# Decode layers with cached attention: the 32-key blocks of K and V in another order over the partitions

## The chip, the core and the metric

The kernel runs on one core of one Trainium2 chip. The metric is the device time of one execution in microseconds (us); a kernel's time is the median of several executions. Durations of single instructions, waits and transfers come from one profiled execution, whose own time stands beside its span below.

## What is computed

Four tokens (B = 4, one new token for each of four sequences, D = 512) go through two identical pairs of layers. The first layer of a pair is attention over a cache: 32 query heads share 8 key/value heads (4 queries to one), each with Sk = 4096 cached keys and values of width Dh = 128. The second is a gated feed-forward layer of width 1792.

```python
def _A_ref(x, k_cache, v_cache, wq, wo):
    q = (x @ wq).reshape(B, Sq, Hq, Dh).transpose(0, 2, 1, 3)
    k = jnp.repeat(k_cache, rep, axis=1)
    v = jnp.repeat(v_cache, rep, axis=1)
    scores = jnp.einsum("bhqd,bhkd->bhqk", q, k) * (Dh ** -0.5)
    p = _softmax(scores, axis=-1)
    o = jnp.einsum("bhqk,bhkd->bhqd", p, v)
    return o.transpose(0, 2, 1, 3).reshape(B, Sq, Hq * Dh) @ wo

x = x + _A_ref(_layernorm(x), k_cache, v_cache, wq, wo)
x = x + _B_ref(_layernorm(x), w_gate, w_up, w_down)
# and the same two lines once more, with the same weights and caches
```

Everything is bf16 in DRAM. K and V of one sequence and one key/value head are 4096 x 128 numbers, 1 MB each. Over the four sequences and eight heads K is 32 MB and V is 32 MB.

The softmax and the sum over the values run over all 4096 keys, so the keys of one head may stand in any order, as long as K and V use the same one.

## The kernel before

K is read from DRAM once and used for both attention layers; V is read twice, once for each attention layer. The work on a head follows one pattern:

- One load brings the 1 MB of a head into one place of `KV`, a buffer of 11 places (`SLOTS`, line 22 and line 337). A place has 128 partitions of 4096 bf16 numbers, 8 KB each: partition p gets 32 consecutive keys, which is one run of 8 KB in DRAM. The keys 32p to 32p+31 are called block p here.
- VectorE transposes the K head in place, in 32 x 32 blocks (`turn`, line 393, its instruction on line 396).
- TensorE computes scores for four heads into one bank of PSUM (`scores`, line 411, its matmuls on line 418). VectorE and ScalarE make the softmax of them (lines 427 to 474), and the probabilities end in `PT` with the same assignment of keys to partitions as K and V have.
- TensorE sums the values (`values`, line 502, its matmuls on line 509), 32 matmuls for a head: each contracts over the 128 partitions, so over 128 blocks, with one key of each.

Heads come by one of two loaders, both of which issue on SyncE's queue. `ld_head` (line 376, the issue on line 379) loads a whole head: 128 partitions of 8 KB. `ld_half` (line 382, the issue on line 385) loads the first or the second 16 keys of each block: 128 partitions of 4 KB out of the 8 KB. All K heads and 16 of the V heads come whole, 48 loads of 1 MB; the other V heads come in halves, 96 loads of 512 KB. For both, the partition is the slowest dimension on both sides of the copy, with 128 entries.

The order of everything is worked out before the program is built. The class `Plan` holds each operation with an engine, a duration, what it needs and what it frees; `loads_k` (line 919) and `loads_v` (line 929) add the loads in a fixed order; `pl.run` (line 1200) chooses the order of issue and the place in `KV` for each load from constants (microseconds per KB and the like). A load is issued when the readers of what stood in its place are done. `spin` (line 1197) fills TensorE's planned gaps with matmuls whose results are not used. None of the plan's inputs says which key goes to which partition.

The last four V heads go to the space of `wq_sb`, which is no longer needed then. At the end come the last output projection, the last feed-forward layer and the stores, about 11 us after the last head has landed.

Of the kernel before, what the change touches and what calls it, by code (L numbers as in the profile page):

```python
# [14 lines left out]
P = 128  # L15
# [36 lines left out]
class Plan:  # L52
# [7 lines left out]
    def add(self, name, eng, dur, deps, emit, acq=(), rel=(), soft=()):  # L60
        assert name not in self.nodes, name
        self.nodes[name] = dict(eng=eng, dur=dur, deps=[d for d in deps if d is not None],
                                emit=emit, acq=acq, rel=rel, soft=list(soft))
        return name
# [191 lines left out]
def kernel(  # L256
# [13 lines left out]
    nc = tc.nc  # L270
# [78 lines left out]
    for z in range(2):  # L349
# [3 lines left out]
                          in_=fold[:].unsqueeze(1).broadcast_to([P, 4, 32]))  # L353
# [9 lines left out]
    def slot(pick):  # L363
        place, h = pick
        whole = wq_sb[:, place[1], :] if isinstance(place, tuple) else KV[:, place, :]
        return whole if h is None else whole[:, 2048 * h:2048 * h + 2048]
# [5 lines left out]
    where = {}  # L372

    def ld_head(name, src):
        def emit(pick):
            where[name] = slot(pick)
            nc.sync.dma_start(out=where[name], in_=src.rearrange("(p c) d -> p (c d)", p=P))
        return emit  # L380

    def ld_half(name, h, src):
        def emit(pick):
            where[name, h] = slot(pick)
            nc.sync.dma_start(out=where[name, h], in_=src.rearrange("(p c) d -> p (c d)", p=P)[:, 2048 * h:2048 * h + 2048])
        return emit

    def keys(name, h):
# [301 lines left out]
    def qtwo_split(z):  # L690
        def emit():
            t = big[:, 256 * z:256 * z + 256].rearrange("p (h x) -> p x h", x=32)
            q = qc[:, z].rearrange("p (f h) -> p f h", f=2)
            nc.vector.scalar_tensor_tensor(out=q, in0=t[:, 2:4], scalar=mneg, in1=t[:, 0:2],
                                           op0=ALU.mult, op1=ALU.add)
            nc.vector.tensor_tensor(out=qs[:, 64 * z:64 * z + 64].rearrange("p (j h) -> p j h", j=4),
                                    in0=qc[:, z:z + 1].broadcast_to([P, 4, 16]),
                                    in1=mask_i.unsqueeze(2).broadcast_to([P, 4, 16]), op=ALU.mult)
        return emit
# [20 lines left out]
    def qsplit(z, b):  # L720
        def emit():
            q = qr[:, z].rearrange("p (k x e) -> p x k e", x=32, e=2)[:, b:b + 1]
            nc.vector.tensor_tensor(out=qs[:, 64 * z:64 * z + 64].rearrange("p (j k e) -> p j k e", j=4, e=2),
                                    in0=q.broadcast_to([P, 4, 8, 2]),
                                    in1=mask_i.unsqueeze(2).unsqueeze(3).broadcast_to([P, 4, 8, 2]), op=ALU.mult)
        return emit
# [3 lines left out]
    def qrep(z):  # L730
        def emit():
            v = slice(64 * z, 64 * z + 64)
            nc.tensor.matmul(Qp[:, v], lhsT=rep[:], rhs=qs[:, v], start=True, stop=True)
        return emit
# [107 lines left out]
    def gelu_b(nb):  # L842
        def emit():
            u = ff(nb)[2]
            nc.scalar.activation(out=u, in_=u, func=ACT.Exp, scale=-2.0 * GELU_C * GELU_A)
            nc.scalar.activation(out=u, in_=u, func=ACT.Ln, bias=ones[:, 1:2])
            nc.scalar.activation(out=u, in_=u, func=ACT.Exp, scale=-1.0)
        return emit
# [25 lines left out]
    def gelu(nb):  # L874
        def emit():
            g = ff(nb)[1]
            nc.scalar.activation(out=g, in_=g, func=ACT.Gelu_apprx_tanh)
        return emit
# [40 lines left out]
    def loads_k(b):  # L919
        for j in range(8):  # L920
            soft = []
            if b and j >= 3:
                soft = [("sc", b - 1, 1, 0 if j < 7 else 1, 1)]
            elif b:
                soft = [("val", b - 2, 1, 5 + j) if b > 1 else ("val", 0, 0, 5 + j)]
            pl.load(("k", b, j), 8, ld_head(("k", b, j), A_k_cache[b, j]), [("sc", b, 1, j // 4, 1)],
                    soft=soft)

    def loads_v(b, L, j0=0, j1=8):
        n = AHEAD.get(b + 1, (0, 0))[1]  # L930
        for j in range(j0, j1):
            if L and j < n:
                soft = [("val", b + 1, 0, AHEAD[b + 1][0] - 3 + j)]
            elif L == 0:
                soft = [("val", b, 0, j - 3) if j >= 3 else (("sc", b - 1, 1, 1, 1) if b else None)]
            elif b == B - 1:
                soft = [("sc", b, 1, 0, 1)]
            else:
                soft = [("val", b + 1, 0, 5 + j - n) if j - n < 3 else ("val", b, 1, j - 3)]
            soft = [x for x in soft if x]  # L940
            name, src = ("v", b, L, j), A_v_cache[b, j]
            if halved(b, L, j):
                pl.load(("vh", b, L, j), 4, ld_half(name, 0, src), [("va", b, L, j)], soft=soft, half=0)
                pl.load(name, 4, ld_half(name, 1, src), [("val", b, L, j)], soft=soft, half=1)
            else:
                pl.load(name, 8, ld_head(name, src), [("val", b, L, j)], soft=soft)
# [97 lines left out]
    for b in range(B):  # L1044
        bs = slice(b, b + 1)
        for L in range(2):
            s = None
            for z in range(2):
                a = ("qx", b, L, z)
                if L:  # L1050
                    p = add(("qs", b, z), "DVE", 0.2 if b else 0.37, [("qt", b, z)], qsplit(z, 0) if b else qtwo_split(z),
                            rel=() if b else (f"big{z}",))
                    p = add(("qp", b, z), "PE", 0.2, [p], qrep(z), acq=("T1",) if z == 0 else ())
# [15 lines left out]
            for z in range(2):  # L1069
                e = (b, L, z)  # L1070
# [11 lines left out]
            if L == 0:  # L1082
# [14 lines left out]
                e = add(("gb", b), "ACT", 0.62, [a], gelu_b(1))  # L1097
# [13 lines left out]
    for b in range(B):  # L1111
        for L in range(2):
            for j in range(8):
# [8 lines left out]
                name, vals = ("v", b, L, j), values2 if pairs else values  # L1122
# [9 lines left out]
                for k, (t0, t1) in enumerate(cuts):  # L1132
                    if t != t1 - 1:
                        continue
                    e = (b, L, z, k)
# [21 lines left out]
    c = add("rowz", "DVE", 0.1, [("of", B - 1, 1, 1, 2)], rows_clear)  # L1157
# [13 lines left out]
    e = add("gset", "ACT", 1.3, [("lnr", "f2")], gelu_table)  # L1171
    e = add("gb2", "ACT", 0.25, [a, e], gelu(B))
    t1 = add("gy2", "DVE", 0.22, [t1], scaled(1, B, rs))
    a = add("gc2", "DVE", 0.22, [e, t1], gelu_c(B))
    c = add("rows", "DVE", 0.7, [end_x, c, a], rows)
# [42 lines left out]
    with tc.manual_schedule():  # L1218
        for name, pick in order:
            e = pl.nodes[name]["emit"]  # L1220
# [36 lines left out]
```

## Time and profile before

| what | value |
|---|---|
| median of 3 runs | 303.39 us (299.53 to 307.93) |
| profiled execution, its own time | 300.37 us |
| profiled execution, span from first to last instruction | 298.4 us |
| mean granted TensorE clock | 0.992 |
| TensorE matmul busy | 230.3 us, 77% (85.5 us of it the largest group of L1197, unused results) |
| VectorE busy | 167.6 us, 56% |
| ScalarE busy | 39.5 us, 13% |
| read from DRAM | 114.56 MB |

The span is the time between the first and the last instruction in the trace; 2.0 us of the execution's own time lie around it. In part 2 of the profile's page the span is cut into 40 equal slices, and each digit is the busy share of a slice in tenths. "SPq" is SyncE's queue, in which the loads are issued; "issue to landing" is the time from such an issue until all of the load's data are in place. "L379" is line 379.

### The profile page before, as it was taken

To read this page: it belongs to the slowest core of one execution; us is meant where nothing else is said; L and a number is where in the kernel's file an instruction comes from. 1 tells how busy PE (TensorE), PEld (TensorE's weight loads), DVE (VectorE), ACT (ScalarE), POOL (GpSimd) and SP (SyncE) were. 2 spreads that over 40 slices of the span, in tenths; PEclk is the share of its full clock that TensorE was granted. 3 is DMA by queue.
4 is the path that set the end of the run, shared out by engine and by line. 5 is a ranking of instruction groups with operands and counts; after the bars stand their busy time and mean duration, and the time that the engine had idled before them with its cause. 6 is when DMAs were issued, how large, how long until landed. Compare 5 with 4: busy or idle time off the path is not lost.

```text
span 298.4 us, 9206 instructions
## 1 busy us (share of the span) xinstructions
PE 230.3 (77%) x4164; PEld 106.4 (36%) x4164; DVE 167.6 (56%) x410; ACT 39.5 (13%) x94; POOL 0.7 (0%) x6
## 2 busy tenths in 40 slices
PE   0197668867896778899876788998777888997965
PEld 0122233322531334454322444454223444544433
DVE  4177963113479893164698941355989622555433
ACT  1020102001020301002203010012112010122102
POOL 0000000000000000000000000000000000000000
PEclk9997999999999999999999999999999999999999
DMA  7999999999989999999999999999999999999910
GB/s 303 404 423 422 421 406 422 399 430 418 419 323 426 376 412 406 405 406 408 380 421 405 406 404 402 406 408 412 408 408 401 412 407 409 404 389 424 419 79 3
DMA packets 23254, 115.15 MB, mean 386 GB/s; under 512 B 2992, under 2 KB 2992, under 8 KB 16560
## 3 DMA queue, kind: packets, MB, share of 16 engines
q1 hardware_dynamic: 23200, 114.57, 95.3%
q8 instruction: 32, 0.52, 0.7%
q14 instruction: 6, 0.05, 0.0%
q10 hardware_dynamic: 16, 0.00, 0.0%
HBM read 114.56 MB, written 0.00 MB: 384 GB/s over the span
## 4 chain that ended last, share of the span: by engine, by line
DMA 70%; PE 18%; DVE 7%; SPq 2%; issue 1%; ACT 0%; DVEq 0%; ACTq 0%
DMA KV<-in_A_v_cache_dram 54%; DMA KV<-in_A_k_cache_dram 8%; DMA wd_sb<-in_B_w_down_dram 7%; PE O_ps L509 5%; PE S_ps L418 4%; DVE KV L396 2%; PE S_ps L1197 2%; PE R_ps L654 2%; PE R_ps L771 1%; DVE big L554 1%; SPq L915 1%; DVE Qb L402 1%; PE S_ps L1190 1%; PE R_ps L809 1%; PE O_ps L563 1%
## 5 line engine op out<-in xcount | busy, mean ns | idle before, releaser
L1197 PE MATMUL S_ps<-iden_b 128*64 128x256 f32 (+5 forms) x238 | 85.5, 457 | 0.0
L396 DVE STREAM_TRANSPOSE KV<-KV 128x1024 int32<-128x1024 int32 x64 | 74.2, 1209 | 1.1 <-DMA KV<-in_A_k_cache_dram 1.0
L509 PE MATMUL O_ps<-KV,PT 128*4 128x128 bf16 x1856 | 43.9, 218 | 21.0 <-DMA KV<-in_A_v_cache_dram 19.6
L509 PEld LDWEIGHTS <-PT 128*4 128x4 bf16 x1920 | 31.9, 83 | 57.0 <-issue 47.0
L418 PE MATMUL S_ps<-KV,Qb 128*32 128x512 bf16 x512 | 38.3, 397 | 12.2 <-DVE KV L396 7.3
L554 DVE STREAM_TRANSPOSE big<-O_ps 128x128 f32<-128x128 f32 (+3 forms) x24 | 12.4, 516 | 45.2 <-PE O_ps L509 43.6
L1197 PEld LDWEIGHTS S_ps<-iden_b 128*64 128x64 f32 x238 | 24.9, 137 | 21.5 <-issue 12.0
L418 PEld LDWEIGHTS <-Qb 128*32 128x32 bf16 x512 | 14.0, 95 | 31.9 <-issue 12.0
L427 DVE TENSOR_REDUCE tiny<-S_ps 128x1 f32<-128x512 f32 x16 | 10.9, 682 | 13.2 <-PE S_ps L418 13.2
L449 ACT ACTIVATE big<-S_ps,bT 128x512 bf16<-128x512 f32 x8 | 5.5, 687 | 89.2 <-DVE bT L441 46.5
L645 ACT ACTIVATE lnt<-lnt 128x1 f32<-128x1 f32 (+1 forms) x10 | 2.0, 203 | 106.9 <-DVE lnt L638 93.2
L589 PE MATMUL R_ps<-XS,tiny 128*128 128x8 f32 (+1 forms) x16 | 3.3, 284 | 13.9 <-DVE XS L580 13.9
L1197 PE MATMUL T_ps<-iden_b 128*64 128x512 f32 (+2 forms) x30 | 13.4, 561 | 0.0
L771 PE MATMUL R_ps<-wo_sb,OT 128*1 128x512 bf16 (+1 forms) x152 | 10.4, 378 | 2.7 <-DMA wo_sb<-in_A_wo_dram 1.8
L466 PE MATMUL T_ps<-big,iden_b 128*32 128x128 bf16 x256 | 6.5, 220 | 7.8 <-DVE big L458 7.6
L474 ACT ACTIVATE PT<-T_ps 128x512 bf16<-128x512 f32 x16 | 9.6, 597 | 19.9 <-PE T_ps L466 15.7
L778 DVE STREAM_TRANSPOSE DA<-R_ps 128x512 f32<-128x512 f32 x8 | 5.7, 711 | 10.7 <-PE R_ps L771 10.7
L458 DVE STREAM_TRANSPOSE big<-big 128x256 int32<-128x256 int32 x16 | 7.0, 440 | 5.3 <-ACT big L449 5.1
L466 PEld LDWEIGHTS <-iden_b 128*32 128x32 bf16 x256 | 4.6, 96 | 14.8 <-issue 10.4
L654 PE MATMUL R_ps<-wq_sb,xz 128*1 128x512 bf16 (+1 forms) x128 | 9.7, 419 | 0.2 <-issue 0.2
L820 DVE STREAM_TRANSPOSE DA<-R_ps 128x448 f32<-128x448 f32 (+1 forms) x10 | 6.0, 601 | 5.2 <-PE R_ps L797 4.4
L449 ACT ACTIVATE big<-S_ps,bT,tiny 128x512 bf16<-128x512 f32 x8 | 6.2, 777 | 18.2 <-DVE bT L441 18.2
(124 smaller groups left out, 157.6 us busy)
## 6 DMA issues: line engine op xcount, KB each, us to landing
KV<-in_A_v_cache_dram SPq DMA_DIRECT2D x96, 512.0 KB, 7.2
KV<-in_A_k_cache_dram SPq DMA_DIRECT2D x32, 1024.0 KB, 12.3
KV<-in_A_v_cache_dram SPq DMA_DIRECT2D x12, 1024.0 KB, 13.4
wq_sb<-in_A_wq_dram SPq DMA_DIRECT2D x1, 4096.0 KB, 12.4
wo_sb<-in_A_wo_dram SPq DMA_DIRECT2D x2, 2048.0 KB, 24.0
wq_sb<-in_A_v_cache_dram SPq DMA_DIRECT2D x4, 1024.0 KB, 13.5
wg_sb<-in_B_w_gate_dram SPq DMA_DIRECT2D x1, 1792.0 KB
wu_sb<-in_B_w_up_dram SPq DMA_DIRECT2D x1, 1792.0 KB, 19.0
```

The costliest lines, as they stand in the source:

```text
L396: nc.vector.transpose(out=w, in_=w)
L418: nc.tensor.matmul(S_ps[z][32 * t:32 * t + 32], lhsT=Qb[:, z, at:at + 32], rhs=kw[t][:, 16 * m:16 * m + 16, je // 2, :, je % 2], start=(m ...
L427: nc.vector.tensor_reduce(out=cms[:, z:z + 1], in_=S_ps[z][:].rearrange("p c r -> p (c r)"), axis=AX.X, op=ALU.max)
L449: nc.scalar.activation(out=Pm[z].bitcast(BF16).rearrange("p (a r e) -> p a r e", a=8, e=2), in_=S_ps[z][:].rearrange("p (a e) r -> p a r e ...
L458: nc.vector.transpose(out=w, in_=w)
L466: nc.tensor.matmul(T_ps[z][32 * i:32 * i + 32, t].rearrange("p (a m x) -> p a m x", a=8, m=2), lhsT=iden_b[:, 32 * t:32 * t + 32], rhs=w[: ...
L474: nc.scalar.activation(out=PT[L][:, z].rearrange("p t a m h e -> p (t a m h e)"), in_=T_ps[z][:].rearrange("p t x -> p (t x)"), func=ACT.Copy)
L509: nc.tensor.matmul(o[32 * g:32 * g + 4, t, :], lhsT=PT[L][:, z, t, c // 2, h, :, c % 2], rhs=vw[:, c, :], start=(h == 0 and n == 0), stop= ...
L554: nc.vector.transpose(out=big[:, P * t0:P * t1].rearrange("p (t j m) -> p t j m", j=4, m=32), in_=o[:, t0:t1, :].rearrange("p t (m j) -> p ...
L654: nc.tensor.matmul(R_ps[z][32 * je:32 * je + nb, :], lhsT=xn[:, c, bs], rhs=w[:, 16 * z:16 * z + 16, je // 2, :, je % 2], start=(c == 0), ...
L771: nc.tensor.matmul(R_ps[0][t:t + nb, :], lhsT=src[:, k, :], rhs=w[:, k, :], start=(k < 4), stop=(k >= n - 4))
L1197: nc.tensor.matmul(sinks[place][0:64, 0:64 * n].rearrange("p (a n) -> p a n", a=n), lhsT=iden_w, rhs=iden_w.unsqueeze(1).broadcast_to([P, ...
```

## The change

Both loaders take the source through a new view, `blocks`. A head's 4096 keys are seen as 8 x 16 x 32 (i, e, c), and the partitions are counted with e outside and i inside: partition 8e + i gets block 16i + e. Partition 0 has block 0 as before, partition 1 has block 16, partition 7 has block 112, partition 8 has block 1, and so on. Each partition still gets one run of 8 KB, or the first or second 4 KB of it. K and V use the same view.

On the source's side the slowest dimension of the copy now has 16 entries (8 KB apart), the next has 8 (128 KB apart); on the side of `KV` there are 128 partitions as before. No instruction is added or taken away on any engine, and the plan is the same; the two issues move from lines 379 and 385 to lines 384 and 390.

```diff
+    def blocks(src):
+        return src.rearrange("(i e c) d -> e i (c d)", i=8, e=16)
+
     def ld_head(name, src):
         def emit(pick):
             where[name] = slot(pick)
-            nc.sync.dma_start(out=where[name], in_=src.rearrange("(p c) d -> p (c d)", p=P))
+            nc.sync.dma_start(out=where[name], in_=blocks(src))
         return emit
 
     def ld_half(name, h, src):
         def emit(pick):
             where[name, h] = slot(pick)
-            nc.sync.dma_start(out=where[name, h], in_=src.rearrange("(p c) d -> p (c d)", p=P)[:, 2048 * h:2048 * h + 2048])
+            nc.sync.dma_start(out=where[name, h], in_=blocks(src)[:, :, 2048 * h:2048 * h + 2048])
         return emit
```

## The prediction

> **What bounds the kernel now.** I read the page from its second part on: first the DMA rows of the 40 slices, then the queues of part 3.
>
> ```profile
> DMA  7999999999989999999999999999999999999910
> GB/s 303 404 423 422 421 406 422 399 430 418 419 323 426 376 412 406 405 406 408 380 421 405 406 404 402 406 408 412 408 408 401 412 407 409 404 389 424 419 79 3
> ...
> q1 hardware_dynamic: 23200, 114.57, 95.3%
> ```
>
> The reader is to see that the 16 DMA engines are busy from the second slice to the 38th, at 400 to 430 GB/s. Then the chain that ended last, part 4 of the page:
>
> ```profile
> DMA 70%; PE 18%; DVE 7%; SPq 2%; issue 1%; ACT 0%; DVEq 0%; ACTq 0%
> ```
>
> The chain is landing, matmuls, next issue, landing. Its PE pieces are the readers whose end frees a place, not a second bound: the engines go on with other queued loads under them. Part 6 gives the sizes.
>
> ```profile
> KV<-in_A_v_cache_dram SPq DMA_DIRECT2D x96, 512.0 KB, 7.2
> KV<-in_A_k_cache_dram SPq DMA_DIRECT2D x32, 1024.0 KB, 12.3
> KV<-in_A_v_cache_dram SPq DMA_DIRECT2D x12, 1024.0 KB, 13.4
> ...
> wq_sb<-in_A_v_cache_dram SPq DMA_DIRECT2D x4, 1024.0 KB, 13.5
> ```
>
> So 96 halves are 50.33 MB and 48 whole heads are 50.33 MB: 100.66 of 114.57 MB go through the two edited loaders. Now the busy time by stretches (the last three columns are granted clock, DMA share and GB/s): whole heads, a stretch where the queue runs thin, halves, the end.
>
> ```profile
> 15.00:35.00 20.00, 15.44 (x102) 4.88 (x102) 16.30 (x25) 3.48 (x7) 0.00 (x0) 0.91 1.01 422
> ...
> 83.00:105.00 22.00, 16.98 (x224) 6.42 (x215) 19.52 (x34) 4.35 (x10) 0.00 (x0) 1.00 0.95 374
> ...
> 165.00:195.00 30.00, 26.06 (x585) 13.40 (x570) 14.07 (x32) 2.38 (x6) 0.00 (x0) 1.00 1.02 405
> ...
> 280.00:298.40 18.40, 12.20 (x324) 6.55 (x323) 6.23 (x27) 1.94 (x4) 0.00 (x0) 0.97 0.28 113
> ```
>
> Whole heads run at 422 GB/s, halves at 405, both with no idle share: the engines are the bound there, about 26 GB/s for each of the 16. The last view is the DMA rows of a short early stretch, 3 to 13 us, with slices of 0.25 us, where `wq_sb` is loaded:
>
> ```profile
> DMA  0099900999039960399303993069900999002799
> GB/s 0 0 524 1180 393 0 0 655 1049 393 0 131 524 1180 262 0 131 655 1180 131 0 131 786 1049 131 0 262 1049 786 0 0 393 918 786 0 0 35 138 434 361
> ```
>
> A transfer is counted where it starts. The reader is to see pulses: the 16 engines begin their long rows nearly together, and for the rest of the period almost nothing begins. A load starts on all engines in step.
>
> **What the change does, part by part.**
>
> *Instructions.* None is added, removed or moved on any engine, and no wait changes. K and V are permuted alike, so scores, softmax and sums do the same work. Cost 0, with nothing needed to hide it.
>
> *Issue on SyncE's queue.* The source has three dimensions instead of two. The trace has these issues:
>
> ```profile
> L385 SPq DMA_DIRECT2D KV<-in_A_v_cache_dram x96: 327/328/791, 86.9 to 259.3; - x96
> ...
> 165.24 32.23 SPq L385 DMA_DIRECT2D KV<-in_A_v_cache_dram  x26
> ```
>
> (min, median and max in ns; then 26 issues in 32.23 us, one per 1.24 us.) The queue is occupied for 0.33 of 1.24 us and waits the rest. The nearest rows with three dimensions are the loads of `wo_sb` and `x_b`, 0.38 to 0.43 us an issue. Lower bound 0; upper, by the longest half's issue, 0.79 us, which still fits under 1.24 us, with seven loads more behind it. Not hidden are the issues in the chain itself (0.49, 0.33, 0.24, 0.60, 0.45 and 0.22 us, 2.3 in all): doubled, +2.3 us. I take 0, by the `wo_sb` rows.
>
> *The reading side.* [...] The gain is bounded by how far the loads are from the best rate in the page, the slice at 430 GB/s: all 100.66 MB at that rate take 234.1 us. Now they take 50.33 MB / 405 GB/s = 124.3 us and 50.33 / 422 = 119.3 us, 243.6 in all. So the gain is between 0 and 9.5 us. I take 0: K heads, with rows one behind the other, and the weights, with rows of up to 32 KB, move at much the same rate, so the order in DRAM does not look like what limits.
>
> *The writing side.* This is what I expect to decide. [...] Now the source counts 16 entries of 8 rows. If each engine takes one entry, as the change wants, engine e must write partitions 8e to 8e+7: the neighbours in DRAM are had by giving the engines other partitions. The trace of before shows only the old assignment, at a rate alike for 4 KB rows, 8 KB rows and weights, so a limit that is the same for all sources and may well lie on the writing side. A new assignment can then only keep that rate or lose it. Bounds from the rows: at best a row takes as long as now (+0). At worst two engines always write through one path and a row takes twice as long: +243.6 us.
>
> Between them: let two engines each write four rows over one path, then four over another. When both are on the same path each goes at half speed. If one leads by f rows, four rows take 8 - f row times: twice the time at f = 0, one and a half at f = 2, none lost at f = 4. Engines start a load in step (the pulses), which speaks for small f; over 150 loads the leads can drift, which speaks for more. I take the middle, f = 2: +0.5 x 243.6 = +121.8 us. Already idle DMA time pays a little back: in the stretch from 83 to 105 us the share is 0.95 where 1.02 is full, 0.07 x 22 = 1.5 us.
>
> [...]
>
> *The sum.* 300.37 + 0 + 0 + 121.8 - 1.5 = 420.7, so **421 us**, against the profiled execution's own 300.37 us (span 298.4, 2.0 around it). The median of the runs shown is 303.39, 1% above. The stretch after the last landing (280 to 298.4 us holds the last rows and some 11 us of compute) stays. When the loads take 1.5 times as long, TensorE, busy 77%, only waits more.
>
> **The rivals.**
>
> *No change.* The engines keep their partitions, or may write any partition at full rate, and the reading side is not the limit. For it: the flat rate over all kinds of source. Against it: to read neighbours together the engines must be given other partitions. Price 0 to +2.3 us (issues in the chain): 297 to 306 us with the scatter of the runs, 301 the likeliest. That the change does not do what it says (each engine keeps its old partitions and reads rows 128 KB apart) ends here too.
>
> *Faster.* DRAM order does cost today: halves, which leave out every other 4 KB, run at 405, whole heads at 422. If neighbours bring everything to 430 GB/s, 9.5 us go: 291 us, 3% less. It decides once all these loads run at 424 GB/s or more (100.66 MB in 237.6 us, 6.0 us or 2% less). Against it: the slices between 165 and 195 us, where halves alone are loaded, show 402 to 406, and whole heads no gain over the weights.
>
> *The issue becomes the bound.* If an issue with three dimensions takes more than a half's time on the engines (512 KB at 405 GB/s = 1.29 us), SyncE's queue sets the pace of 96 halves: at 1.5 us, 96 x 0.21 = 20 us, so 321 us. Against it: every three-dimensional issue in the trace takes under 0.45 us.
>
> *A write-side loss that is small.* Leads settle near f = 4: at f = 3.5 rows take 4.5/4, +30 us, 331 us. The two together are "slower, but little", 308 to 345 us.
>
> **How the numbers follow.** Large write-side loss: 0.62, its own range 349 us (f = 3.2, x1.2) to 543 us (x2). Slower by little: 0.12. No change: 0.18. Faster: 0.08. The prediction is the first's 421 us. The range goes from 298, which takes in nearly all of "no change", to 513 us (f = 0.5: 0.875 x 243.6 = +213 us); left out are "faster" and the top of the first case, under 0.2. Faster by over 2%: 0.08; within 2% (about what a measurement of this kernel, with 299.5 to 307.9 over three runs, can tell from none): 0.18; slower by over 2%: 0.74.
>
> **What would show it.** The DMA rows of the slices: still 9 everywhere, but 220 to 340 GB/s where K and V are loaded and still about 420 where `wo_sb`, `wg_sb` and `wu_sb` are (first 80 us). A share of 9 with fewer GB/s means rows that take longer; a share that falls means late issues, seen as longer issues on line 390. Issue to landing of halves would rise from 7.2 to 10 us and more. TensorE's granted clock may fall, as its waits lengthen. I am wrong if the rate of the halves stays at 405 GB/s or rises, and wrong in size if it leaves 220 to 340.

## The result and the profile after

| kernel | median | runs |
|---|---|---|
| before | 301.46 us | 299.53 to 307.93, 6 runs |
| changed | 450.6 us | 442.56 to 462.88, 6 runs |
| changed / before | 1.479 | 95% interval 1.471 to 1.488 |

The changed kernel takes half as long again. Its runs scatter by 4.6%; the ratio goes by those close to its fastest, and the profiled execution (462.88 us, span 461.0) is its slowest, so its stretches overstate the loss a little.

First the DMA rows of the 40 slices and the queue's row of the changed kernel's page, as they were shown of the kernel before. A slice is now 11.5 us.

```profile
DMA  9999999999999999999999999999999999999950
GB/s 364 220 227 228 227 293 229 232 406 334 240 233 231 257 256 260 269 272 260 248 242 248 261 252 250 247 248 249 242 252 264 267 280 275 266 248 235 233 144 2
...
q1 hardware_dynamic: 23200, 114.57, 97.4%
```

The engines are as busy as before (97.4% of 16 engines' span; 95.3% before), with the same 23200 packets and the same 114.57 MB, and move 220 to 280 GB/s where K and V alone are loaded. The peak of 406 in the ninth slice is the weights, which do not go through the new view. The engines do not run out of work: each transfer of K and V takes longer. By the single rows in the trace, a row of 8 KB takes 550 ns on average where it took 319, and one of 4 KB 251 where it took 164 (some rows of weights have these sizes and are counted in); the weights' rows of 32 KB take 1307 ns (1303 before). The chain and the loads:

```profile
DMA 89%; PE 9%; DVE 1%; SPq 1%; issue 0%
...
KV<-in_A_v_cache_dram SPq DMA_DIRECT2D x96, 512.0 KB, 11.7
KV<-in_A_k_cache_dram SPq DMA_DIRECT2D x32, 1024.0 KB, 24.3
KV<-in_A_v_cache_dram SPq DMA_DIRECT2D x12, 1024.0 KB, 18.9
```

The chain is now 89% DMA (70 before). Halves take 11.7 us from issue to landing (7.2 before), K heads 24.3 (12.3). The busy time by stretches (last three columns: granted TensorE clock, DMA share, GB/s), whole heads first, then a stretch with halves alone:

```profile
20.00:60.00 40.00, 15.50 (x105) 5.58 (x105) 19.41 (x25) 1.63 (x4) 0.00 (x0) 0.71 1.01 227
...
150.00:205.00 55.00, 36.27 (x666) 17.34 (x667) 15.01 (x38) 3.12 (x9) 0.00 (x0) 0.79 1.03 262
```

Whole heads run at 227 GB/s in the first stretch where they ran at 422, which makes a row take 1.86 times as long; halves at 262 in the second where they ran at 405, 1.55 times. TensorE's clock is 0.71 to 0.79 there. Last, the issues on SyncE's queue (duration in ns, min/median/max):

```profile
L390 SPq DMA_DIRECT2D KV<-in_A_v_cache_dram x96: 536/537/1523, 125.5 to 401.6; - x96
```

An issue takes 537 ns where it took 328.

### The profile page after: what moved, and what is told of

Same layout as the page of the kernel before. It is cut to its first block, busy times and chain, and to the rows that moved or that the text cites. A ratio compares the mean times of both kernels' runs of the same rounds, so it can differ in the third digit from the quotient of the medians.

```text
span 461.0 us, 9206 instructions
## 1 busy us (share of the span) xinstructions
PE 278.4 (60%) x4164; PEld 122.6 (27%) x4164; DVE 169.4 (37%) x410; ACT 39.4 (9%) x94; POOL 0.7 (0%) x6
## 3 DMA queue, kind: packets, MB, share of 16 engines
q1 hardware_dynamic: 23200, 114.57, 97.4%
## 4 chain that ended last, share of the span: by engine, by line
DMA 89%; PE 9%; DVE 1%; SPq 1%; issue 0%
DMA KV<-in_A_v_cache_dram 68%; DMA KV<-in_A_k_cache_dram 14%; DMA wd_sb<-in_B_w_down_dram 6%; PE O_ps L514 3%; PE S_ps L1202 1%; PE S_ps L423 1%; PE R_ps L673 1%; PE R_ps L814 1%; PE R_ps L659 1%; PE R_ps L776 0%; SPq L384 0%; PE R_ps L891 0%; DVE Qb L407 0%; DVE big L559 0%; PE R_ps L751 0%
## 5 line engine op out<-in xcount | busy, mean ns | idle before, releaser
L514 PE MATMUL O_ps<-KV,PT 128*4 128x128 bf16 x1856 | 52.3, 247 | 105.3 <-DMA KV<-in_A_v_cache_dram 104.2
L1202 PE MATMUL S_ps<-iden_b 128*64 128x256 f32 (+5 forms) x238 | 103.1, 537 | 0.0
L401 DVE STREAM_TRANSPOSE KV<-KV 128x1024 int32<-128x1024 int32 x64 | 75.5, 1217 | 42.4 <-DMA KV<-in_A_k_cache_dram 42.4
L514 PEld LDWEIGHTS <-PT 128*4 128x4 bf16 x1920 | 38.3, 92 | 157.2 <-issue 140.5
L423 PE MATMUL S_ps<-KV,Qb 128*32 128x512 bf16 x512 | 40.2, 428 | 35.2 <-DVE Qb L407 20.4
L1202 PEld LDWEIGHTS S_ps<-iden_b 128*64 128x64 f32 x238 | 28.5, 158 | 25.8 <-issue 18.6
L1202 PE MATMUL T_ps<-iden_b 128*64 128x512 f32 (+2 forms) x30 | 17.8, 719 | 0.0
L776 PE MATMUL R_ps<-wo_sb,OT 128*1 128x512 bf16 (+1 forms) x152 | 15.3, 525 | 0.9 <-DVE OT L575 0.8
L659 PE MATMUL R_ps<-wq_sb,xz 128*1 128x512 bf16 (+1 forms) x128 | 11.1, 479 | 0.0
L1195 PE MATMUL S_ps<-iden_b 128*128 128x256 bf16 (+1 forms) x26 | 9.1, 349 | 0.0
## 6 DMA issues: line engine op xcount, KB each, us to landing
KV<-in_A_v_cache_dram SPq DMA_DIRECT2D x96, 512.0 KB, 11.7
KV<-in_A_k_cache_dram SPq DMA_DIRECT2D x32, 1024.0 KB, 24.3
```

The lines of the kernel that those rows point to most:

```text
L401: nc.vector.transpose(out=w, in_=w)
L423: nc.tensor.matmul(S_ps[z][32 * t:32 * t + 32], lhsT=Qb[:, z, at:at + 32], rhs=kw[t][:, 16 * m:16 * m + 16, je // 2, :, je % 2], start=(m ...
L514: nc.tensor.matmul(o[32 * g:32 * g + 4, t, :], lhsT=PT[L][:, z, t, c // 2, h, :, c % 2], rhs=vw[:, c, :], start=(h == 0 and n == 0), stop= ...
L659: nc.tensor.matmul(R_ps[z][32 * je:32 * je + nb, :], lhsT=xn[:, c, bs], rhs=w[:, 16 * z:16 * z + 16, je // 2, :, je % 2], start=(c == 0), ...
L776: nc.tensor.matmul(R_ps[0][t:t + nb, :], lhsT=src[:, k, :], rhs=w[:, k, :], start=(k < 4), stop=(k >= n - 4))
L1195: nc.tensor.matmul(sinks[place][:, 0:P * n].rearrange("p (a n) -> p a n", a=n), lhsT=iden_b[:], rhs=iden_b[:].unsqueeze(1).broadcast_to([P ...
```

## The experiments

The theory is that of the prediction: the new view cuts the copy otherwise among the engines, so that pairs of them meet while they write; in step both go at half speed, four rows apart they do not meet, and eight rows apart they do again. That is the author's supposition, the partners four numbers apart included: no view of the profile shows which engine writes which partition, or what two engines would share. The runs test what would follow. The rivals are the reading side (neighbours in DRAM read together are slow), the issue, and TensorE's lower clock.

**The neighbours without the new cut.** The source gets 32 entries of 4 rows, with the entries still 8 KB apart. The author supposed that rows which run together are then still neighbours in DRAM, and that the copy is cut among the engines as before; no view shows either.

```diff
-        return src.rearrange("(i e c) d -> e i (c d)", i=8, e=16)
+        return src.rearrange("(i e c) d -> e i (c d)", i=4, e=32)
```

> The source's view has 32 entries of 4 rows instead of 16 of 8: partitions 4g to 4g+3 get blocks g, 32+g, 64+g, 96+g. [...] Writing side (my theory: the change is slow because two engines write into the same groups of partitions): 298 to 305 us, halves at 400 GB/s or more. Reading side (rival: neighbours in DRAM read together are slow): 400 us or more, halves at 300 GB/s or less. If neighbours help and the writing side is as before: 291 to 297 us.

Measured: 302.71 us (12 runs), 1.007 times the kernel before, interval 1.003 to 1.010. Its stretches:

```profile
15.00:35.00 20.00, 16.21 (x103) 4.98 (x102) 16.16 (x24) 3.45 (x7) 0.00 (x0) 0.91 1.01 423
...
165.00:195.00 30.00, 25.19 (x549) 12.63 (x551) 15.15 (x29) 2.23 (x5) 0.00 (x0) 1.00 1.03 407
```

423 and 407 GB/s, as before (422 and 405). Only from 83 to 135 us it is a little slower (363 and 397 GB/s in the stretches from 83 and 105 us, 374 and 407 before), which the run on the issue below shows too (362 and 390). This order in DRAM costs nothing beyond that, and gains nothing that this run shows. If the supposition on the rows holds, the reading side is not what made the change slow.

**The new cut without the neighbours.** There are 16 entries of 8 rows, as in the change. The blocks stand in the old order over the partitions, but each row starts 256 B before the end of the one before it.

```diff
-        return src.rearrange("(i e c) d -> e i (c d)", i=8, e=16)
+        return bass.AP(src.tensor, src.offset, [[8 * 4096, 16], [3968, 8], [1, 4096]])
```

> [...] Each row starts 256 B before the end of the row before it, so some keys are read twice and others not at all. Writing side: as slow as the changed kernel, 440 to 465 us. Reading side: 300 to 306 us.

Measured: 462.2 us (440.22 to 464.81, 4 runs), as slow as the change. Its early stretches:

```profile
20.00:35.00 15.00, 4.57 (x23) 1.49 (x22) 6.80 (x8) 0.00 (x0) 0.00 (x0) 0.69 1.02 227
35.00:60.00 25.00, 11.40 (x86) 4.11 (x81) 11.86 (x18) 1.38 (x3) 0.00 (x0) 0.70 1.01 225
```

The same 227 GB/s, with the old order in DRAM. The two runs together put the loss on the new cut (227 GB/s with 16 entries of 8 rows, 423 with 32 of 4) and not on the order in DRAM; that the cut acts through the partitions that each engine writes is the theory's reading of it, and not shown.

**A lead of four rows.** If two engines of a pair meet only because they run in step, a head start of four rows must undo it. The changed kernel gets two extra loads after `x_b`, into a place of `KV` that is filled later anyway:

```diff
+                if name == "x":
+                    rows = blocks(A_k_cache[0, 0])
+                    for _ in range(1):
+                        nc.sync.dma_start(out=KV[0:16, 9, :], in_=rows[0:4, 0:4, :])
+                        nc.sync.dma_start(out=KV[32:80, 9, :], in_=rows[0:12, 0:4, :])
```

> The changed kernel with two short extra loads ahead of the first K head: one that runs on 4 engines and one that runs on 12, four rows of 8 KB for each engine. If the extra loads go to the engines with the lowest numbers, engines 0 to 3 then run four rows behind engines 4 to 7, and 8 to 11 four rows behind 12 to 15. Writing side with pairs (e, e+4) that each write four rows into one group and four into the other: with a lead of four rows a pair never meets, so from 20 to 60 us the rate is 350 to 425 GB/s where the changed kernel has 227, and the time falls by 20 to 40 us, to 405 to 430. With halves, whose rows take half as long, the lead is eight rows and helps no more. Reading side: engines four rows apart still read neighbours, 227 GB/s in that stretch, and the time stays at 443 to 463 us plus 2.

Measured: 437.94 us (427.08 to 445.48, 4 runs).

```profile
20.00:35.00 15.00, 9.88 (x45) 3.06 (x45) 10.67 (x12) 0.01 (x1) 0.00 (x0) 0.77 1.01 405
...
35.00:44.00 9.00, 5.66 (x61) 2.31 (x62) 8.83 (x14) 1.38 (x3) 0.00 (x0) 1.00 1.03 399
44.00:50.00 6.00, 2.11 (x50) 1.04 (x50) 2.79 (x8) 0.00 (x0) 0.00 (x0) 1.00 0.98 274
50.00:55.00 5.00, 4.95 (x56) 2.21 (x55) 1.61 (x6) 0.70 (x3) 0.00 (x0) 0.66 1.06 299
```

The same loads, with the same view, run at about 400 instead of 227 GB/s from 20 to 44 us. The leads can be seen in the trace, which has 16 transfers of 4 B for each load: in the changed kernel all 16 fall within 1.2 us at the end of each load of 4.6 us; here, from 20 to 35 us, they come in two groups of eight, half a load apart.

From 44 us on the rows of `wo_sb`, whose view is not the new one, run between those of the heads, and the lead is no longer worth as much: 274 GB/s then, 299 and 292 behind it. Why it is lost no run here tried. So the effect is there in full and ends sooner than expected, and the time falls by 13 us between the medians, not by 20 to 40 (450.6 to 437.94; the two kernels' times overlap between 442.56 and 445.48).

**A lead of eight rows.** The same extra loads twice, into two places:

```diff
-                    for _ in range(1):
-                        nc.sync.dma_start(out=KV[0:16, 9, :], in_=rows[0:4, 0:4, :])
-                        nc.sync.dma_start(out=KV[32:80, 9, :], in_=rows[0:12, 0:4, :])
+                    for k in range(2):
+                        nc.sync.dma_start(out=KV[0:16, 9 - k, :], in_=rows[0:4, 0:4, :])
+                        nc.sync.dma_start(out=KV[32:80, 9 - k, :], in_=rows[0:12, 0:4, :])
```

> The same with both extra loads twice, so a lead of eight rows, one whole load. Writing side: the pairs meet at every row again, 220 to 250 GB/s from 25 to 60 us, time 445 to 465 us. If instead any lead is good (a start in step is what hurts), the rate is 350 GB/s or more as with four rows. Reading side: 227 GB/s, 445 to 465 us.

Measured: 468.99 us (445.97 to 475.56, 4 runs).

```profile
20.00:35.00 15.00, 4.01 (x9) 1.31 (x8) 3.35 (x5) 0.00 (x0) 0.00 (x0) 0.66 1.02 228
35.00:60.00 25.00, 9.41 (x58) 3.09 (x59) 13.76 (x17) 1.38 (x3) 0.00 (x0) 0.71 1.01 230
```

Four rows ahead: 405. Eight rows ahead, a whole load: 228. It is not the start in step as such but the place in the load that decides; that four rows help and eight do not is what the theory's pairs would give. The median lies above the 445 to 465 us expected; the rate, which decides here, does not leave its range.

**A lead for half the pairs.** Only the extra load on 4 engines, so that by the theory half of the pairs get no lead:

```diff
-                        nc.sync.dma_start(out=KV[32:80, 9, :], in_=rows[0:12, 0:4, :])
```

> [...] Pairs (e, e+4): a load is done when its slowest pair is, so 225 to 250 GB/s from 25 to 60 us, as without a lead. If a lead of some engines is enough: 350 GB/s or more.

Measured: 451.84 us (one run).

```profile
20.00:35.00 15.00, 4.57 (x10) 1.51 (x10) 6.58 (x8) 0.00 (x0) 0.00 (x0) 0.68 1.03 232
35.00:60.00 25.00, 11.84 (x94) 4.46 (x93) 13.78 (x20) 1.38 (x3) 0.00 (x0) 0.70 1.01 229
```

The rate is the one expected, but pairs that are independent of each other do not explain it. The lead is there: from 20 to 35 us the 4-byte transfers of each load come in a group of 4 and a group of 12, about half a load apart. By such pairs eight of the engines should then write their rows in some 310 ns and idle until the others are done, so the share should fall. But the share is 1.03, and no 8 KB row that starts from 20 to 35 us takes less than 459 ns (309 to 322 ns in the kernel before, 309 to 365 with both extra loads). All 16 engines are slow, those with the lead too. Why, stays open: what the runs show is nearly the full rate with eight engines half a load apart from the other eight (405 GB/s), and about half of it with 16 together (227) or with 12 and 4 (232).

Which engines are partners is not shown either, nor which of them an extra load takes: the groups of 4 and 12 show how many, and no view here shows their numbers. That they are those with the lowest numbers was the author's supposition; with it, partners four numbers apart fit, and partners eight apart would have had the same leads.

**The issue alone.** The kernel before, with one switch of the builder set, under which the issue of a half takes 472 ns instead of 328:

```diff
     nc = tc.nc
+    nc.dge_precook = False
```

> The kernel before with nothing changed but the form in which every load is issued: the longer one, 0.54 us on SyncE's queue instead of 0.33, which the new view brings with it. If that is the 2 us by which the 32 x 4 view is slower than before: 301.5 to 304 us. If the issue is hidden: 299.5 to 301.5 us. If the issue were what made the change slow: 400 us or more.

Measured: 303.4 us (302.23 to 308.26, 10 runs), 1.010 times the kernel before, interval 1.007 to 1.014. An issue, and the stretch where the queue runs thin:

```profile
L386 SPq DMA_DIRECT2D KV<-in_A_v_cache_dram x96: 471/472/797, 88.1 to 261.9; - x96
```

```profile
83.00:105.00 22.00, 17.60 (x223) 6.54 (x216) 18.99 (x37) 4.11 (x10) 0.00 (x0) 1.00 0.91 362
...
165.00:195.00 30.00, 25.66 (x553) 12.94 (x552) 15.84 (x31) 3.29 (x7) 0.00 (x0) 1.00 1.03 409
```

At 0.47 us an issue it costs 3 us. Where loads queue up it is hidden (409 GB/s from 165 to 195 us, 405 before); where the queue runs thin it is not (share 0.91 and 362 GB/s from 83 to 105 us, 0.95 and 374 before). That stretch is not all of it: from 105 to 135 us this run has 390 GB/s at a share of 1.02, where 407 and 1.03 stood before, and no view here sorts out the 3 us. It accounts for the size of what the 32 x 4 view is slower by; the two intervals overlap, so whether that view gains something in reading on top stays open.

**The clock.** The changed kernel without the matmuls of `spin`:

```diff
-            if name in gaps:
-                spin(*gaps[name])
```

> The changed kernel without the matmuls that fill TensorE's gaps, so that its granted clock falls further. If the transfers alone set the time: 440 to 465 us. If part of the slowdown is TensorE's lower clock (0.81 to 0.84 in the changed kernel, 0.99 before): 470 us or more.

Measured: 452.46 us (444.22 to 455.05, 4 runs), 1.491 times the kernel before, interval 1.477 to 1.505.

```profile
PEclk9955565555575555655865556588555566669566
```

```profile
20.00:60.00 40.00, 7.54 (x82) 2.83 (x82) 20.25 (x27) 1.38 (x3) 0.00 (x0) 0.52 1.02 227
```

The mean granted clock falls from 0.81 to 0.62, the whole heads stay at 227 GB/s, the time stays (452.46 us, 450.6 with the filling). So TensorE's lower clock costs nothing here. From 150 to 205 us this run has 240 GB/s (262 in the changed kernel); the clock is no reason for that, since the same run has 345 GB/s from 280 to 300 us at a clock of 0.54.

**Reading, tried the other way.** In the kernel before, a half of a V head as one piece of DRAM (the values are then summed with the probabilities of other keys):

```diff
-            nc.sync.dma_start(out=where[name, h], in_=src.rearrange("(p c) d -> p (c d)", p=P)[:, 2048 * h:2048 * h + 2048])
+            nc.sync.dma_start(out=where[name, h], in_=src.rearrange("(h p c) d -> h p (c d)", h=2, p=P)[h])
```

> [...] If neighbours in DRAM help reading at all, halves come nearer to 412 GB/s (4 KB in the shortest row time) from 405: 297 to 299 us. If DRAM order costs nothing here: 300 to 301.5 us.

Measured: 299.02 us (12 runs), 0.996 times the kernel before, interval 0.993 to 1.000. The halves run at 407 to 409 GB/s in the stretches from 105, 165 and 225 us, where they had 407, 405 and 408. About 1 us, barely clear of nothing.

The version of it that computes the reference gives the same keys to K and to the whole V heads, in two pieces of 4 KB a partition:

```diff
-            nc.sync.dma_start(out=where[name], in_=src.rearrange("(p c) d -> p (c d)", p=P))
+            nc.sync.dma_start(out=where[name], in_=src.rearrange("(h p c) d -> p h (c d)", h=2, p=P))
```

> The kernel before with the key order that lets a half of V be one piece of 512 KB, now for K and the whole V heads too, so that the output is the reference's: each partition has 16 keys of the first and 16 of the second half of a head. Whole heads then come in rows of 4 KB instead of 8. If the row length costs what it does in the kernel before (405 against 422 GB/s): 50.33 MB take up to 5 us longer and the halves give back about 1, so 301 to 305 us. If a whole head in two pieces runs at the whole heads' rate: 298.5 to 300 us, a little better than before.

Measured: 301.91 us (12 runs), 1.004 times the kernel before, interval 1.001 to 1.007; whole heads at 410 GB/s from 15 to 35 us (422 before). What the halves gain, the shorter rows of the whole heads take. No version tried that computes the reference beats the kernel before.

## Why the prediction was right, point by point

- *Instructions.* Held: nothing but the loads and what waits for them changed. VectorE is busy for 169.4 us (167.6 before); TensorE's 278.4 (230.3) come with a lower clock (0.81 on average, 0.992 before).
- *Issue, taken as 0.* With the loads at full rate the longer issue costs about 2 to 3 us (1.007 times the kernel before with 32 entries of 4 rows, 1.010 with the builder's switch), so the rival "no change", priced at 0 to +2.3 us, was priced a little low. In the changed kernel, whose engines are busy for 97.4% of the span, no run separates what it costs. The nearest rows were chosen by the number of dimensions (`wo_sb`, `x_b`, 0.38 to 0.43 us), but with the builder's switch an issue costs 0.47 us for loads with two dimensions too, and through the new views it costs 0.54. The bound for issues in the chain, +2.3 us for a doubled issue, left out at least the stretch where the queue runs thin; 0.14 us more an issue already cost 3. As a rival for the bound it was rightly set aside: 0.54 is well under a half's 1.29 us.
- *Reading side, taken as 0, at most 9.5 us.* Right: two orders meant to bring more neighbours together ran at 397 to 423 GB/s where the DMA share was full, gaining 0.4% at best. The argument was that rates alike for all kinds of source point away from DRAM.
- *Writing side, +121.8 us.* That the new cut costs up to half of the rate (227 GB/s for 422), and that the engines' leads decide how much (405 with four rows, 228 with eight), is shown by the runs on the cut and the leads. No run shows the term itself, a path that two engines share, nor that the new view gives the engines other partitions; in its place the runs showed these rates. That it happens in pairs is not shown, and the run with a lead for half the pairs (232 GB/s) speaks against pairs that are independent. The size was too small: a lead of two rows was taken for all loads, by choice of the middle. By the prediction's own formula turned round, 8 - f = 4 x 1.86 gives f = 0.6 for whole heads in the first 60 us, and 4 x 1.55 gives f = 1.8 for halves from 150 to 205 us. That the halves came near the middle is luck; whole heads run nearly in step (16 transfers of 4 B within 1.2 us), which the pulses in the trace of before had spoken for. In time: 50.33 MB at 262 GB/s and 50.33 MB at 227 are 192 + 222 = 414 us, 170 more than 243.6. Over the whole trace the 8 KB rows take 1.72 times as long (550 to 319 ns) and those of 4 KB 1.53 times (251 to 164 ns), and the profiled execution lost 462.88 - 300.37 = 162.5. This term is why 421 us is 7% under the median of 450.6.
- *Idle time paid back, -1.5 us.* Of that size: about 2.6% of 461.0 us is idle, 12.0 us, against 4.7% of 298.4 us, 14.0 us.
- *The range, 298 to 513 us.* It holds "no change" too, so the time alone says little for the mechanism. The rates and the runs with leads say more.
- *What would show it.* As said: share 9 everywhere, 220 to 340 GB/s with K and V, weights at their old rate (rows of 32 KB in 1307 ns, 1303 before), longer landings, a lower clock that costs nothing.

## What to carry to other kernels

In these runs the rate of the loads went with the outermost count on the source's side: with 16 there they lost up to 46% of their rate (422 to 227 GB/s) at a full DMA share, in both orders tried; with 32 (423 GB/s) or 128 (422) the rate was whole. That this count sets how a copy is cut into shares for the 16 DMA engines is the author's reading of it. When a load's view changes, look at GB/s beside the share, and reorder the source only in views whose outermost count has kept the rate in a run.

## What the runs showed that I had not expected

- The rate of the same loads went with how far single engines were ahead of each other: 405 GB/s with a lead of four rows and 228 with eight. Leads also seem to arise by themselves. In the run without filling, whose loads are those of the changed kernel, the page shows three slices above 320 in the middle; in the run with a lead for half the pairs there are such slices late in the span, where the changed kernel has 250 to 280:

```profile
GB/s 364 217 228 225 226 274 256 229 375 368 227 213 223 232 240 238 241 245 242 256 273 277 261 276 328 343 323 244 255 269 259 256 255 257 268 265 245 242 143 3
...
GB/s 352 236 227 229 231 253 260 243 360 378 249 193 221 228 237 237 243 245 244 245 232 236 242 292 316 322 324 290 237 240 245 305 322 325 324 282 240 241 122 2
```

  In the first of these runs, from 280 to 300 us (345 GB/s), the 4-byte transfers of the halves stand in two groups half a load apart, 106 and 102 of them; from 160 to 180 us (237 GB/s) 133 of 147 stand together. This may be what makes the changed kernel's runs scatter by 4.6%; it was not tried.
- One more 0.14 us an issue, on a queue that is occupied a quarter of the time (0.33 of 1.24 us), cost 1% (303.4 us, 1.010 times).
